# A decode layer on one core: one W_o set loaded as 64 rows, and 48 of 128 score columns by TensorE in the last step

## The chip, the cores and the metric

The kernel runs on one core of one Trainium2 chip. The metric is the device time of one execution in microseconds, as the median of the runs shown. The profile is of one more execution of the same program, read from the first to the last instruction (its span).

## The reference

One token for each of two sequences goes through an attention layer with a key and value cache and then through a gated feed-forward layer, all in bfloat16:

```
q = layernorm(x) @ wq                     # B=2, D=512, 32 heads of 128
scores = q . k_cache / sqrt(128)          # 8192 cached positions per head
p = softmax(scores);  o = p . v_cache
h = x + o @ wo
g = layernorm(h)
out = h + (relu(g @ W_gate) * (g @ W_up)) @ W_down     # F=1376
```

There are 32 key and value heads, one for each query head. The K and V caches are 134 MB each, read once; the weights are some 12 MB. No number of the caches is used twice.

## The kernel before

**Steps.** The work on the caches goes in 32 steps (`steps`), 16 pairs of heads for each of the two sequences. A step takes 4 MB of K and 4 MB of V. Each of the 128 partitions holds 128 consecutive positions (`NT`) of one head: the first 64 partitions have the pair's first head, the other 64 its second. K and V have two buffers each (`kbuf`, `vbuf`), and step i uses buffer i % 2. All loads are issued from SyncE's queue by `load_kv` (line 115): the K of step i+2 after `scores(i)`, the V of step i+1 after the second half of the values of step i-1.

**Scores.** The 128 score columns of a step are shared. The last `NPE` = 32 go through TensorE (`scores_pe`): eight positions' tiles are transposed against an identity (line 268), ScalarE copies the eight from PSUM to SBUF (`kT`, line 269), and eight matmuls with q follow (line 259). There are four such groups, and two copies bring their scores into `scol` (lines 277 and 278). The first `NV` = 96 columns go through VectorE: a product of K with q, which is written over K (`products`, line 286), and in `scores` four halving adds (line 301) and a sum over the last eight elements (line 305). Then come the maximum over the columns (line 310), over the partitions with a matmul (line 312) and a minimum (line 317), and the exponentials on ScalarE (line 320).

**Values.** `values(i, part)` multiplies the probabilities with V in two halves of 16 matmuls (line 336). For the last two steps `values_cols` does it in 128 narrow matmuls (line 359).

**The order.** It is written out by hand (`tc.manual_schedule`): every engine runs its instructions in the order in which the program gives them. In the loop at the end of the kernel's middle part step i gives: `scores_pe(i)`, `products(i)`, `behind(i - 2)`, the first half of the values of step i-1, `scores(i)`, the next K load, the second half of the values, the next V load. In the last step (31) `values_cols(30)` stands between `behind(29)` and `scores(31)`.

**behind.** Some steps close a group of head pairs. For them `sums` adds the exponentials over the partitions with a matmul (line 236, `z_ps`) and takes the reciprocal on VectorE (line 238), and `normalise` scales the group's outputs (line 242). Where the heads of a whole W_o set are then known, `attend_set` multiplies them with W_o.

**W_o.** It lies in `wbig`, where W_q was, in three sets of 16, 8 and 4 heads (`SETS`) and the last four heads by themselves. In a set of n heads each of the 128 partitions holds n consecutive rows of W_o, so that each partition gets one contiguous run of n KB; the loads are at line 196. The heads' outputs must then be brought to the partitions which hold their rows. `attend_set` spreads them with a product (line 373) and a matmul with a pattern of ones (`quot` and `rest`, line 377), copies that to SBUF (line 381), and multiplies with W_o's rows, four matmuls for each row index (line 384). The last four heads are loaded head by head and multiplied by `attend` (line 392).

**The end.** After step 31 there are the last values, the attention's sum with x (line 454), the second layer norm (`ln_cols`), the gate and up products (line 463) and the down product (line 478). W_gate and W_up go into the first K buffer after the last use of that buffer in step 30, and W_down is loaded in four pieces, the last one of 96 rows (64, 24 and 8) in the middle of the run (line 432).

Of the kernel before, what the change touches and what calls it, by code (L numbers as in the profile page):

```python
# [7 lines left out]
ACT = mybir.ActivationFunctionType  # L8
ALU = mybir.AluOpType
# [14 lines left out]
def kernel(  # L24
# [24 lines left out]
    ROW = NT * Dh  # L49
    NG = Hq // 2  # L50
    NPE = NT // 4
    NV = NT - NPE
    TPC = 8
    VG = 4
    EPS = 1e-5
# [5 lines left out]
    FC = 11  # L61


    SETS = [(0, Hq // 2), (Hq // 2, Hq // 4), (3 * Hq // 4, Hq // 8)]
    HM = Hq - Hq // 8

    assert Sq == 1 and Hkv == Hq and Dh == P and D == KC * P and Hq == 32 and NPE % TPC == 0
    assert F == 10 * P + 96

    consts = ctx.enter_context(tc.tile_pool(name="consts", bufs=1))  # L70
# [4 lines left out]

    kbuf = big.tile([P, 2, ROW], bf16)
    vbuf = big.tile([P, 2, ROW], bf16)
    wbig = big.tile([P, KC * Hq * Dh], bf16)
    wd_sb = big.tile([P, FC, D], bf16)
    qrep = consts.tile([P, B, NG, Dh], bf16)  # L80

    wq_sb = wbig.rearrange("p (c n) -> p c n", c=KC)
    wo_sb = wbig.rearrange("p (h n) -> p h n", h=Hq)

    wgu = kbuf[:, 0, 0:2 * KC * F].rearrange("p (k c f) -> p k c f", k=2, c=KC)

# [11 lines left out]
    warm = consts.tile([P, 1], f32)  # L98
    ocol = consts.tile([P, Hq, B], bf16)

    quot = [consts.tile([P, P // n], bf16, name=f"quot{n}") for _, n in SETS]
    rest = [consts.tile([P, n], bf16, name=f"rest{n}") for _, n in SETS]
    orow = [consts.tile([P, n, B], bf16, name=f"orow{n}") for _, n in SETS]
    qT = consts.tile([P, B, Hq], bf16)
    xc = consts.tile([P, B, KC], f32)
    hc = consts.tile([P, B, KC], f32)
# [31 lines left out]
    with tc.manual_schedule():  # L138

        xb = small.tile([P, B, KC], bf16, tag="xb")  # L140
        nc.sync.dma_start(out=xb, in_=_dram(A_x, 0, [[KC, P], [D, B], [1, KC]]))
        nc.sync.dma_start(out=wbig, in_=_dram(A_wq, 0, [[KC * Hq * Dh, P], [1, KC * Hq * Dh]]))
        load_kv(A_k_cache, kbuf, 0, pieces=4)
        load_kv(A_k_cache, kbuf, 1)
        load_kv(A_v_cache, vbuf, 0)
# [46 lines left out]
                nc.scalar.activation(out=qrep[:, b, g0:g0 + 4, :], in_=r_ps, func=ACT.Copy)  # L192


        for h0, n in SETS:
            nc.sync.dma_start(
                out=wbig[:, h0 * D:(h0 + n) * D], in_=_dram(A_wo, h0 * Dh * D, [[n * D, P], [1, n * D]]),
            )
        nc.sync.dma_start(
            out=wo_sb[:, HM:Hq, :], in_=_dram(A_wo, HM * Dh * D, [[D, P], [Dh * D, Hq - HM], [1, D]]),  # L200
        )
        for (h0, n), qu, re in zip(SETS, quot, rest):
            nc.gpsimd.memset(re, 0.0)
            for k in range(P // n):
                nc.gpsimd.affine_select(  # L205
                    out=re, in_=re, compare_op=ALU.not_equal, fill=1.0,
                    base=-k * n, pattern=[[-1, n]], channel_multiplier=1,
                )
            nc.gpsimd.memset(qu, 1.0)
            nc.gpsimd.affine_select(  # L210
                out=qu, in_=qu, compare_op=ALU.is_ge, fill=0.0,
                base=0, pattern=[[-n, P // n]], channel_multiplier=1,
            )
            nc.gpsimd.affine_select(
                out=qu, in_=qu, compare_op=ALU.is_ge, fill=0.0,
                base=n - 1, pattern=[[n, P // n]], channel_multiplier=-1,
            )


# [25 lines left out]

        scols = {}

        def scores_pe(i):
            b, g = steps[i]
            s = i % 2  # L250
            kt = kbuf[:, s, :]

            sc_ps = ps.tile([P, NPE, 2], f32, tag="sc")
            kT = small.tile([P, NPE * P], bf16, tag="kT")

            def times_q(c0):
                for k in range(TPC):
                    t = c0 + k
                    nc.tensor.matmul(  # L259
                        out=sc_ps[:, t, :], lhsT=kT[:, t * P:(t + 1) * P],  # L260
                        rhs=qT[:, b, 2 * g:2 * g + 2], start=True, stop=True,
                    )

            for c0 in range(0, NPE, TPC):
                t_ps = ps2.tile([P, TPC, P], bf16, tag="tp")
                for k in range(TPC):
                    t = NV + c0 + k
                    nc.tensor.transpose(t_ps[:, k, :], kt[:, t * Dh:(t + 1) * Dh], ident)  # L268
                nc.scalar.activation(  # L269
                    out=kT[:, c0 * P:(c0 + TPC) * P], in_=t_ps.rearrange("p t s -> p (t s)"), func=ACT.Copy,  # L270
                )
                if c0:
                    times_q(c0 - TPC)
            times_q(NPE - TPC)
            scol = small.tile([P, NT], f32, tag="scol")
            scols[i] = scol
            nc.scalar.activation(out=scol[0:HALF, NV:NT], in_=sc_ps[0:HALF, :, 0], func=ACT.Copy)  # L277
            nc.scalar.activation(out=scol[HALF:P, NV:NT], in_=sc_ps[HALF:P, :, 1], func=ACT.Copy)

        def products(i):  # L280

            b, g = steps[i]
            kt = kbuf[:, i % 2, :]
            for t0, n in ([(0, 32), (32, 32), (64, 32)] if i == 0 else [(0, NV)]):
                kv = _free(kt, t0 * Dh, [[Dh, n], [1, Dh]])
                nc.vector.tensor_tensor(  # L286
                    out=kv, in0=kv,
                    in1=_free(qrep, (b * NG + g) * Dh, [[0, n], [1, Dh]]), op=ALU.mult,
                )

        def scores(i):

            b, g = steps[i]
            s = i % 2
            kt = kbuf[:, s, :]
            scol = scols[i]
            width = Dh
            while width > 8:
                half = width // 2
                lo = _free(kt, 0, [[Dh, NV], [1, half]])  # L300
                nc.vector.tensor_tensor(  # L301
                    out=lo, in0=lo, in1=_free(kt, half, [[Dh, NV], [1, half]]), op=ALU.add,
                )
                width = half
            nc.vector.tensor_reduce(  # L305
                out=scol[:, 0:NV], in_=_free(kt, 0, [[Dh, NV], [1, 8]]), axis=AXIS.X, op=ALU.add,
            )

            pm = small.tile([P, 1], f32, tag="pm")
            nc.vector.tensor_reduce(out=pm, in_=scol, axis=AXIS.X, op=ALU.max)  # L310
            mx_ps = ps.tile([P, 2, HALF], f32, tag="mx")
            nc.tensor.matmul(  # L312
                out=mx_ps.rearrange("p a b -> p (a b)"), lhsT=_free(pm, 0, [[0, P]]), rhs=nscale,
                start=True, stop=True,
            )
            nm = small.tile([P, 2], f32, tag="nm")
            nc.vector.tensor_reduce(out=nm, in_=mx_ps, axis=AXIS.X, op=ALU.min)  # L317
            for j in range(2):
                r = slice(j * HALF, (j + 1) * HALF)
                nc.scalar.activation(  # L320
                    out=pgz[r, s, :, j, :], in_=scol[r, :].rearrange("p (u t) -> p u t", t=VG), func=ACT.Exp, scale=SCALE,
                    bias=nm[r, j:j + 1], accum_out=zc[r, b, g, j:j + 1],
                )
# [41 lines left out]

        def attend_set(k):

            h0, n = SETS[k]
            or_ps = ps.tile([P, B, n], f32, tag="mx")
            for b in range(B):  # L370
                sp = small.tile([P, P], bf16, tag="spread")
                nq = P // n
                nc.vector.tensor_tensor(
                    out=_free(sp, 0, [[nq, n], [1, nq]]), in0=_free(ocol, h0 * B + b, [[B, n], [0, nq]]),
                    in1=_free(quot[k], 0, [[0, n], [1, nq]]), op=ALU.mult,
                )
                nc.tensor.matmul(
                    out=or_ps[:, b, :], lhsT=sp, rhs=rest[k],
                    start=True, stop=True,
                )  # L380
            nc.scalar.activation(out=orow[k], in_=or_ps.rearrange("p b c -> p c b"), func=ACT.Copy)
            for r in range(n):
                for c in range(KC):
                    nc.tensor.matmul(
                        out=att_ps[:, c, :],
                        lhsT=_free(wo_sb, (h0 + r) * D + c, [[KC, P]]), rhs=orow[k][:, r, :],
                        start=(h0 == 0 and r == 0 and c == 0), stop=False, skip_group_check=True,
                    )

        def attend(h):  # L390
            for c in range(KC):
                nc.tensor.matmul(
                    out=att_ps[:, c, :],
                    lhsT=_free(wo_sb, h * D + c, [[KC, P]]), rhs=ocol[:, h, :],
                    start=False, stop=(h == Hq - 1), skip_group_check=True,
                )

        def behind(i):
# [4 lines left out]
            normalise(i)  # L403
            b, g0, n = groups[i]
            if b == B - 1:
                for k, (h0, m) in enumerate(SETS):
                    if 2 * (g0 + n) == h0 + m:
                        attend_set(k)
                if 2 * g0 >= HM:
                    for h in range(2 * g0, 2 * (g0 + n)):  # L410
                        attend(h)
# [103 lines left out]
```

## Time and profile before

| | |
|---|---|
| Median of 3 runs | 670.48 us (670.46 to 671.56) |
| The profiled execution | 671.36 us |
| Its span | 669.6 us |
| Mean granted TensorE clock | 0.784 of full speed |
| Read from HBM | 281.05 MB, 420 GB/s over the span |
| PE busy | 444.4 us (66%) |
| VectorE (DVE) busy | 478.5 us (71%) |
| ScalarE (ACT) busy | 195.9 us (29%) |
| GpSimd (POOL) busy | 26.2 us (4%) |

The share of busy time is a mean over the span. A line of the timeline or of the chain gives the start in us from the span's start and the length in us; then the engine, the line of the kernel (L286 is line 286), the operation, what it writes and reads with shapes, the count, and in brackets the engine's idle time before it and what ended that. The chain of waits is followed back from the last instruction: at each step to what released it, or to the instruction before it on its engine.

### The profile page before, as it was taken

Reading aid. Unit: us, or ns where it says so; the run is one execution under the profiler, and the core shown is the slowest. Engines: PE = TensorE matmul, PEld = TensorE weight load, DVE = VectorE, ACT = ScalarE, POOL = GpSimd, SP = SyncE. Lnnn points to the kernel's source line nnn. Section 1 sums busy time; section 2 is a strip of 40 time slices with the busy share of each in tenths; the row PEclk is TensorE's granted clock in tenths of the full one; section 3 lists DMA queues with packets and bytes.
Section 4 is the critical chain, followed back from the end, with each engine's and each line's share of the span. In section 5 each row is a group of like instructions: output and inputs, shape, how many; then the busy total and the mean of one; then the engine's idle time right before and its main releaser. Section 6 shows DMA issues by size and latency. Waiting matters only on the chain.

```text
span 669.6 us, 8843 instructions
## 1 busy us (share of the span) xinstructions
PE 444.4 (66%) x3878; PEld 230.3 (34%) x3878; DVE 478.5 (71%) x301; ACT 195.9 (29%) x372; POOL 26.2 (4%) x84
## 2 busy tenths in 40 slices
PE   2563765677666668776656776666776866588655
PEld 2432332333223333332323332333333433343255
DVE  1891788777778767778877776887777788777771
ACT  1531233333212333222233321323331223333130
POOL 7800000000000000000000000000000000000000
PEclk9857678988767788876789877778887767798775
DMA  8999999999999999999999999999999999999994
GB/s 349 433 419 428 437 436 426 431 428 430 437 424 430 415 434 426 439 426 432 428 430 432 431 434 422 435 430 430 430 431 434 428 426 431 438 430 426 427 412 167
DMA packets 12618, 281.62 MB, mean 421 GB/s; under 512 B 1860, under 2 KB 2468, under 8 KB 2980
## 3 DMA queue, kind: packets, MB, share of 16 engines
q1 hardware_dynamic: 12580, 281.06, 98.2%
q8 instruction: 30, 0.49, 0.3%
q14 instruction: 8, 0.07, 0.0%
HBM read 281.05 MB, written 0.00 MB: 420 GB/s over the span
## 4 chain that ended last, share of the span: by engine, by line
DMA 67%; PE 21%; DVE 10%; ACT 1%; issue 0%; SPq 0%; DVEq 0%
DMA vbuf<-in_A_v_cache_dram 53%; PE pv_ps L336 18%; DMA kbuf<-in_A_k_cache_dram 12%; DVE kbuf L301 5%; DVE kbuf L286 4%; DMA wbig<-in_A_wq_dram 2%; PE mx_ps L312 1%; DVE scol L305 1%; ACT kT L269 1%; PE q_ps L176 1%; PE o_ps L359 1%; PE g_ps L463 0%; PE d_ps L478 0%; PE u_ps L463 0%; PE z_ps L236 0%
## 5 line engine op out<-in xcount | busy, mean ns | idle before, releaser
L336 PE MATMUL pv_ps<-vbuf,pgz 128*8 128x512 bf16 x960 | 281.9, 460 | 122.1 <-DMA vbuf<-in_A_v_cache_dram 122.1
L286 DVE TENSOR_TENSOR kbuf<-kbuf,qrep 128x12288 bf16<-128x12288 bf16 (+1 forms) x34 | 210.0, 6181 | 119.7 <-DMA kbuf<-in_A_k_cache_dram 106.7
L301 DVE TENSOR_TENSOR kbuf<-kbuf 128x6144 bf16<-128x6144 bf16 (+3 forms) x128 | 212.1, 1657 | 4.2
L336 PEld LDWEIGHTS <-pgz 128*8 128x8 bf16 x960 | 93.3, 100 | 286.7 <-issue 215.6
L269 ACT ACTIVATE kT<-t_ps 128x1024 bf16<-128x1024 bf16 x128 | 124.2, 1021 | 32.4 <-PE t_ps L268 32.0
L320 ACT ACTIVATE pgz<-scol,nm 64x128 bf16<-64x128 f32 x64 | 25.5, 399 | 327.6 <-DVE nm L317 326.9
L268 PE MATMUL t_ps<-ident,kbuf 128*128 128x128 bf16 x1024 | 77.4, 227 | 16.9 <-DMA kbuf<-in_A_k_cache_dram 16.9
L259 PE MATMUL sc_ps<-qT,kT 128*128 128x2 bf16 x1024 | 45.4, 165 | 48.3 <-ACT kT L269 45.5
L268 PEld LDWEIGHTS <-kbuf 128*128 128x128 bf16 x1024 | 62.4, 102 | 27.4 <-DMA kbuf<-in_A_k_cache_dram 25.6
L259 PEld LDWEIGHTS <-kT 128*128 128x128 bf16 x1024 | 34.7, 97 | 67.5 <-ACT kT L269 67.5
L317 DVE TENSOR_REDUCE nm<-mx_ps 128x2 f32<-128x128 f32 x32 | 9.3, 292 | 39.8 <-PE mx_ps L312 39.8
L343 ACT ACTIVATE pv<-pv_ps 8x512 f32<-8x512 f32 x30 | 17.7, 589 | 64.6 <-PE pv_ps L336 64.6
L305 DVE TENSOR_REDUCE scol<-kbuf 128x96 f32<-128x768 bf16 x32 | 30.5, 953 | 1.1
L312 PE MATMUL mx_ps<-nscale,pm 128*128 128x128 f32 x64 | 16.2, 336 | 7.0 <-DVE pm L310 6.9
L312 PEld LDWEIGHTS mx_ps<-nscale,pm 128*128 128x128 f32 x64 | 9.9, 194 | 20.3 <-issue 11.7
L205 POOL TENSOR_SCALAR_AFFINE_SELECT rest<-rest 128x4 bf16<-128x4 bf16 (+2 forms) x56 | 16.7, 299 | 4.0 <-POOL rest L205 0.2
L348 PE MATMUL o_ps<-pick,pv 128*128 128x8 f32 (+1 forms) x64 | 8.4, 258 | 5.5 <-ACT pv L343 5.5
L320 ACT ACTIVATION_READ_ACCUMULATOR pgz<-scol,nm 64x1 f32 x64 | 11.8, 185 | 0.0
L310 DVE TENSOR_REDUCE pm<-scol 128x1 f32<-128x128 f32 x32 | 9.2, 286 | 3.3
L348 PEld LDWEIGHTS o_ps<-pick,pv 128*128 128x128 f32 x64 | 7.7, 191 | 9.5 <-ACT pv L343 8.3
L277 ACT ACTIVATE scol<-sc_ps 64x32 f32<-64x32 f32 x32 | 6.1, 191 | 14.3 <-PE sc_ps L259 14.3
L176 PE MATMUL q_ps<-xn,wbig 128*128 128x2 bf16 x128 | 3.6, 165 | 8.7 <-DMA wbig<-in_A_wq_dram 8.7
(71 smaller groups left out, 94.5 us busy)
## 6 DMA issues: line engine op xcount, KB each, us to landing
kbuf<-in_A_k_cache_dram SPq DMA_DIRECT2D x31, 4096.0 KB, 24.6
vbuf<-in_A_v_cache_dram SPq DMA_DIRECT2D x31, 4096.0 KB, 29.3
wbig<-in_A_wq_dram SPq DMA_DIRECT2D x1, 4096.0 KB, 12.9
kbuf<-in_A_k_cache_dram SPq DMA_DIRECT2D x4, 1024.0 KB, 18.2
vbuf<-in_A_v_cache_dram SPq DMA_DIRECT2D x4, 1024.0 KB, 18.5
wbig<-in_A_wo_dram SPq DMA_DIRECT2D x1, 2048.0 KB
kbuf<-in_B_W_gate_dram SPq DMA_DIRECT2D x1, 1376.0 KB
kbuf<-in_B_W_up_dram SPq DMA_DIRECT2D x1, 1376.0 KB
```

The costliest lines, as they stand in the source:

```text
L205: nc.gpsimd.affine_select(out=re, in_=re, compare_op=ALU.not_equal, fill=1.0, base=-k * n, pattern=[[-1, n]], channel_multiplier=1,)
L259: nc.tensor.matmul(out=sc_ps[:, t, :], lhsT=kT[:, t * P:(t + 1) * P], rhs=qT[:, b, 2 * g:2 * g + 2], start=True, stop=True,)
L268: nc.tensor.transpose(t_ps[:, k, :], kt[:, t * Dh:(t + 1) * Dh], ident)
L269: nc.scalar.activation(out=kT[:, c0 * P:(c0 + TPC) * P], in_=t_ps.rearrange("p t s -> p (t s)"), func=ACT.Copy,)
L286: nc.vector.tensor_tensor(out=kv, in0=kv, in1=_free(qrep, (b * NG + g) * Dh, [[0, n], [1, Dh]]), op=ALU.mult,)
L301: nc.vector.tensor_tensor(out=lo, in0=lo, in1=_free(kt, half, [[Dh, NV], [1, half]]), op=ALU.add,)
L305: nc.vector.tensor_reduce(out=scol[:, 0:NV], in_=_free(kt, 0, [[Dh, NV], [1, 8]]), axis=AXIS.X, op=ALU.add,)
L312: nc.tensor.matmul(out=mx_ps.rearrange("p a b -> p (a b)"), lhsT=_free(pm, 0, [[0, P]]), rhs=nscale, start=True, stop=True,)
L320: nc.scalar.activation(out=pgz[r, s, :, j, :], in_=scol[r, :].rearrange("p (u t) -> p u t", t=VG), func=ACT.Exp, scale=SCALE, bias=nm[r, j ...
L336: nc.tensor.matmul(out=pv_ps[i][r, :], lhsT=pgz[:, s, u].rearrange("p j t -> p (j t)"), rhs=vbuf[:, s, u * VG * Dh:(u + 1) * VG * Dh], sta ...
L343: nc.scalar.activation(out=pv[r, w], in_=pv_ps[i][r, :], func=ACT.Copy)
L348: nc.tensor.matmul(out=o_ps[i][:, 0:2 * n], lhsT=pv[:, w, t * Dh:(t + 1) * Dh], rhs=pick[:, t, first % 4:first % 4 + n].rearrange("p k j - ...
```

## The change

Two things are changed, with what they need.

The set of 8 heads is laid on 64 partitions: each holds 16 rows of W_o instead of 8. A set is now described by its first head, its number of heads, the partitions it lies on and its first column in `wbig`, and `SROWS` gives the rows in a partition (16, 16 and 4). In the load of the 64-partition set, DRAM rows are taken in the order of an outer dimension of eight and an inner one of eight, so that the transfer's source has eight as its slowest dimension. The spread's pattern and the matmuls of `attend_set` follow: the sums are over 64 partitions, and there are 16 row indices instead of 8. `wbig` becomes 40 x 512 columns wide instead of 32 x 512, and the last four heads lie from column 36 x 512 on.

In the last step 48 columns of scores go through TensorE and 80 through VectorE (`NPE_LAST`, `share`); in the others it remains 32 and 96. The tile `kT` of a whole step becomes one tile for each group of eight, of which there are four buffers.

```diff
-    NV = NT - NPE
+    NPE_LAST = 3 * NT // 8
...
-    SETS = [(0, Hq // 2), (Hq // 2, Hq // 4), (3 * Hq // 4, Hq // 8)]
+    SETS = [(0, 16, P, 0), (16, 8, HALF, 20), (24, 4, P, 16)]
+    WO_T = 36
...
-    wbig = big.tile([P, KC * Hq * Dh], bf16)
+    wbig = big.tile([P, 40 * D], bf16)
...
+    SROWS = [n * Dh // w for _, n, w, _ in SETS]
+    quot = [consts.tile([P, Dh // r], bf16, name=f"quot{k}") for k, r in enumerate(SROWS)]
+    rest = [consts.tile([P, r], bf16, name=f"rest{k}") for k, r in enumerate(SROWS)]
+    orow = [consts.tile([P, r, B], bf16, name=f"orow{k}") for k, r in enumerate(SROWS)]
...
-        for h0, n in SETS:
+        for (h0, n, w, at), r in zip(SETS, SROWS):
+            rows = [[r * D, w]] if w == P else [[r * D, 8], [8 * r * D, w // 8]]
             nc.sync.dma_start(
-                out=wbig[:, h0 * D:(h0 + n) * D], in_=_dram(A_wo, h0 * Dh * D, [[n * D, P], [1, n * D]]),
+                out=wbig[0:w, at * D:(at + r) * D], in_=_dram(A_wo, h0 * Dh * D, rows + [[1, r * D]]),
             )
...
-        for (h0, n), qu, re in zip(SETS, quot, rest):
+        for r, qu, re in zip(SROWS, quot, rest):
             nc.gpsimd.memset(re, 0.0)
-            for k in range(P // n):
+            for k in range(P // r):
...
+        def share(i):
+
+            npe = NPE_LAST if i == N - 1 else NPE
+            return NT - npe, npe
+
         def scores_pe(i):
...
-            kT = small.tile([P, NPE * P], bf16, tag="kT")
+            kTs = {}
...
-            for c0 in range(0, NPE, TPC):
+            for c0 in range(0, npe, TPC):
                 t_ps = ps2.tile([P, TPC, P], bf16, tag="tp")
                 for k in range(TPC):
-                    t = NV + c0 + k
+                    t = nv + c0 + k
                     nc.tensor.transpose(t_ps[:, k, :], kt[:, t * Dh:(t + 1) * Dh], ident)
-                nc.scalar.activation(
-                    out=kT[:, c0 * P:(c0 + TPC) * P], in_=t_ps.rearrange("p t s -> p (t s)"), func=ACT.Copy,
-                )
+                kTs[c0] = small.tile([P, TPC * P], bf16, tag="kT", name="kT", bufs=4)
+                nc.scalar.activation(out=kTs[c0], in_=t_ps.rearrange("p t s -> p (t s)"), func=ACT.Copy)
...
-                lo = _free(kt, 0, [[Dh, NV], [1, half]])
+                lo = _free(kt, 0, [[Dh, nv], [1, half]])
...
         def attend_set(k):
 
-            h0, n = SETS[k]
-            or_ps = ps.tile([P, B, n], f32, tag="mx")
+            h0, n, w, at = SETS[k]
+            r = SROWS[k]
+            nq = Dh // r
+            or_ps = ps.tile([P, B, r], f32, tag="mx")
             for b in range(B):
                 sp = small.tile([P, P], bf16, tag="spread")
-                nq = P // n
                 nc.vector.tensor_tensor(
-                    out=_free(sp, 0, [[nq, n], [1, nq]]), in0=_free(ocol, h0 * B + b, [[B, n], [0, nq]]),
+                    out=_free(sp, 0, [[nq, n], [1, nq]] if w == P else [[1, n], [8, nq]]),
+                    in0=_free(ocol, h0 * B + b, [[B, n], [0, nq]]),
                     in1=_free(quot[k], 0, [[0, n], [1, nq]]), op=ALU.mult,
                 )
...
-            for r in range(n):
+            for c0 in range(r):
                 for c in range(KC):
                     nc.tensor.matmul(
                         out=att_ps[:, c, :],
-                        lhsT=_free(wo_sb, (h0 + r) * D + c, [[KC, P]]), rhs=orow[k][:, r, :],
-                        start=(h0 == 0 and r == 0 and c == 0), stop=False, skip_group_check=True,
+                        lhsT=_free(wbig[0:w], (at + c0) * D + c, [[KC, P]]), rhs=orow[k][0:w, c0, :],
+                        start=(k == 0 and c0 == 0 and c == 0), stop=False, skip_group_check=True,
                     )
```

More of the change, by code (lines that the diff above doesn't have):

```diff
@@ L61 @@
     FC = 11
-    SETS = [(0, Hq // 2), (Hq // 2, Hq // 4), (3 * Hq // 4, Hq // 8)]
+    SETS = [(0, 16, P, 0), (16, 8, HALF, 20), (24, 4, P, 16)]
+    WO_T = 36
     HM = Hq - Hq // 8
-    assert Sq == 1 and Hkv == Hq and Dh == P and D == KC * P and Hq == 32 and NPE % TPC == 0
+    assert Sq == 1 and Hkv == Hq and Dh == P and D == KC * P and Hq == 32 and NPE % TPC == NPE_LAST % TPC == 0
     assert F == 10 * P + 96
@@ L77 @@
     vbuf = big.tile([P, 2, ROW], bf16)
-    wbig = big.tile([P, KC * Hq * Dh], bf16)
+    wbig = big.tile([P, 40 * D], bf16)
     wd_sb = big.tile([P, FC, D], bf16)
     qrep = consts.tile([P, B, NG, Dh], bf16)
-    wq_sb = wbig.rearrange("p (c n) -> p c n", c=KC)
-    wo_sb = wbig.rearrange("p (h n) -> p h n", h=Hq)
+    wq_sb = wbig[:, 0:KC * Hq * Dh].rearrange("p (c n) -> p c n", c=KC)
     wgu = kbuf[:, 0, 0:2 * KC * F].rearrange("p (k c f) -> p k c f", k=2, c=KC)
@@ L99 @@
     ocol = consts.tile([P, Hq, B], bf16)
-    quot = [consts.tile([P, P // n], bf16, name=f"quot{n}") for _, n in SETS]
-    rest = [consts.tile([P, n], bf16, name=f"rest{n}") for _, n in SETS]
-    orow = [consts.tile([P, n, B], bf16, name=f"orow{n}") for _, n in SETS]
+    SROWS = [n * Dh // w for _, n, w, _ in SETS]
+    quot = [consts.tile([P, Dh // r], bf16, name=f"quot{k}") for k, r in enumerate(SROWS)]
+    rest = [consts.tile([P, r], bf16, name=f"rest{k}") for k, r in enumerate(SROWS)]
+    orow = [consts.tile([P, r, B], bf16, name=f"orow{k}") for k, r in enumerate(SROWS)]
     qT = consts.tile([P, B, Hq], bf16)
@@ L141 @@
         nc.sync.dma_start(out=xb, in_=_dram(A_x, 0, [[KC, P], [D, B], [1, KC]]))
-        nc.sync.dma_start(out=wbig, in_=_dram(A_wq, 0, [[KC * Hq * Dh, P], [1, KC * Hq * Dh]]))
+        nc.sync.dma_start(out=wbig[:, 0:KC * Hq * Dh], in_=_dram(A_wq, 0, [[KC * Hq * Dh, P], [1, KC * Hq * Dh]]))
         load_kv(A_k_cache, kbuf, 0, pieces=4)
@@ L192 @@
                 nc.scalar.activation(out=qrep[:, b, g0:g0 + 4, :], in_=r_ps, func=ACT.Copy)
-        for h0, n in SETS:
+        for (h0, n, w, at), r in zip(SETS, SROWS):
+            rows = [[r * D, w]] if w == P else [[r * D, 8], [8 * r * D, w // 8]]
             nc.sync.dma_start(
-                out=wbig[:, h0 * D:(h0 + n) * D], in_=_dram(A_wo, h0 * Dh * D, [[n * D, P], [1, n * D]]),
+                out=wbig[0:w, at * D:(at + r) * D], in_=_dram(A_wo, h0 * Dh * D, rows + [[1, r * D]]),
             )
         nc.sync.dma_start(
-            out=wo_sb[:, HM:Hq, :], in_=_dram(A_wo, HM * Dh * D, [[D, P], [Dh * D, Hq - HM], [1, D]]),
+            out=wbig[:, WO_T * D:(WO_T + Hq - HM) * D].rearrange("p (h n) -> p h n", n=D),
+            in_=_dram(A_wo, HM * Dh * D, [[D, P], [Dh * D, Hq - HM], [1, D]]),
         )
-        for (h0, n), qu, re in zip(SETS, quot, rest):
+        for r, qu, re in zip(SROWS, quot, rest):
             nc.gpsimd.memset(re, 0.0)
-            for k in range(P // n):
+            for k in range(P // r):
                 nc.gpsimd.affine_select(
                     out=re, in_=re, compare_op=ALU.not_equal, fill=1.0,
-                    base=-k * n, pattern=[[-1, n]], channel_multiplier=1,
+                    base=-k * r, pattern=[[-1, r]], channel_multiplier=1,
                 )
@@ L211 @@
                 out=qu, in_=qu, compare_op=ALU.is_ge, fill=0.0,
-                base=0, pattern=[[-n, P // n]], channel_multiplier=1,
+                base=0, pattern=[[-r, P // r]], channel_multiplier=1,
             )
@@ L215 @@
                 out=qu, in_=qu, compare_op=ALU.is_ge, fill=0.0,
-                base=n - 1, pattern=[[n, P // n]], channel_multiplier=-1,
+                base=r - 1, pattern=[[r, P // r]], channel_multiplier=-1,
             )
@@ L251, in scores_pe @@
             kt = kbuf[:, s, :]
-            sc_ps = ps.tile([P, NPE, 2], f32, tag="sc")
-            kT = small.tile([P, NPE * P], bf16, tag="kT")
+            nv, npe = share(i)
+            sc_ps = ps.tile([P, npe, 2], f32, tag="sc")
+            kTs = {}
             def times_q(c0):
                 for k in range(TPC):
-                    t = c0 + k
                     nc.tensor.matmul(
-                        out=sc_ps[:, t, :], lhsT=kT[:, t * P:(t + 1) * P],
+                        out=sc_ps[:, c0 + k, :], lhsT=kTs[c0][:, k * P:(k + 1) * P],
                         rhs=qT[:, b, 2 * g:2 * g + 2], start=True, stop=True,
                     )
-            for c0 in range(0, NPE, TPC):
+            for c0 in range(0, npe, TPC):
                 t_ps = ps2.tile([P, TPC, P], bf16, tag="tp")
                 for k in range(TPC):
-                    t = NV + c0 + k
+                    t = nv + c0 + k
                     nc.tensor.transpose(t_ps[:, k, :], kt[:, t * Dh:(t + 1) * Dh], ident)
-                nc.scalar.activation(
-                    out=kT[:, c0 * P:(c0 + TPC) * P], in_=t_ps.rearrange("p t s -> p (t s)"), func=ACT.Copy,
-                )
+                kTs[c0] = small.tile([P, TPC * P], bf16, tag="kT", name="kT", bufs=4)
+                nc.scalar.activation(out=kTs[c0], in_=t_ps.rearrange("p t s -> p (t s)"), func=ACT.Copy)
                 if c0:
                     times_q(c0 - TPC)
-            times_q(NPE - TPC)
+            times_q(npe - TPC)
             scol = small.tile([P, NT], f32, tag="scol")
             scols[i] = scol
-            nc.scalar.activation(out=scol[0:HALF, NV:NT], in_=sc_ps[0:HALF, :, 0], func=ACT.Copy)
-            nc.scalar.activation(out=scol[HALF:P, NV:NT], in_=sc_ps[HALF:P, :, 1], func=ACT.Copy)
+            nc.scalar.activation(out=scol[0:HALF, nv:NT], in_=sc_ps[0:HALF, :, 0], func=ACT.Copy)
+            nc.scalar.activation(out=scol[HALF:P, nv:NT], in_=sc_ps[HALF:P, :, 1], func=ACT.Copy)
         def products(i):
@@ L283, in products @@
             kt = kbuf[:, i % 2, :]
-            for t0, n in ([(0, 32), (32, 32), (64, 32)] if i == 0 else [(0, NV)]):
+            nv, _ = share(i)
+            for t0, n in ([(0, 32), (32, 32), (64, 32)] if i == 0 else [(0, nv)]):
                 kv = _free(kt, t0 * Dh, [[Dh, n], [1, Dh]])
@@ L296, in scores @@
             scol = scols[i]
+            nv, _ = share(i)
             width = Dh
@@ L299, in scores @@
                 half = width // 2
-                lo = _free(kt, 0, [[Dh, NV], [1, half]])
+                lo = _free(kt, 0, [[Dh, nv], [1, half]])
                 nc.vector.tensor_tensor(
-                    out=lo, in0=lo, in1=_free(kt, half, [[Dh, NV], [1, half]]), op=ALU.add,
+                    out=lo, in0=lo, in1=_free(kt, half, [[Dh, nv], [1, half]]), op=ALU.add,
                 )
@@ L305, in scores @@
             nc.vector.tensor_reduce(
-                out=scol[:, 0:NV], in_=_free(kt, 0, [[Dh, NV], [1, 8]]), axis=AXIS.X, op=ALU.add,
+                out=scol[:, 0:nv], in_=_free(kt, 0, [[Dh, nv], [1, 8]]), axis=AXIS.X, op=ALU.add,
             )
@@ L366, in attend_set @@
         def attend_set(k):
-            h0, n = SETS[k]
-            or_ps = ps.tile([P, B, n], f32, tag="mx")
+            h0, n, w, at = SETS[k]
+            r = SROWS[k]
+            nq = Dh // r
+            or_ps = ps.tile([P, B, r], f32, tag="mx")
             for b in range(B):
                 sp = small.tile([P, P], bf16, tag="spread")
-                nq = P // n
                 nc.vector.tensor_tensor(
-                    out=_free(sp, 0, [[nq, n], [1, nq]]), in0=_free(ocol, h0 * B + b, [[B, n], [0, nq]]),
+                    out=_free(sp, 0, [[nq, n], [1, nq]] if w == P else [[1, n], [8, nq]]),
+                    in0=_free(ocol, h0 * B + b, [[B, n], [0, nq]]),
                     in1=_free(quot[k], 0, [[0, n], [1, nq]]), op=ALU.mult,
                 )
[L377 to L381, printed above, removed]
-            for r in range(n):
+                nc.tensor.matmul(out=or_ps[0:w, b, :], lhsT=sp[:, 0:w], rhs=rest[k], start=True, stop=True)
+            nc.scalar.activation(
+                out=orow[k][0:w], in_=or_ps[0:w].rearrange("p b c -> p c b"), func=ACT.Copy,
+            )
+            for c0 in range(r):
                 for c in range(KC):
@@ L393, in attend @@
                     out=att_ps[:, c, :],
-                    lhsT=_free(wo_sb, h * D + c, [[KC, P]]), rhs=ocol[:, h, :],
+                    lhsT=_free(wbig, (WO_T + h - HM) * D + c, [[KC, P]]), rhs=ocol[:, h, :],
                     start=False, stop=(h == Hq - 1), skip_group_check=True,
@@ L405, in behind @@
             if b == B - 1:
-                for k, (h0, m) in enumerate(SETS):
+                for k, (h0, m, _, _) in enumerate(SETS):
                     if 2 * (g0 + n) == h0 + m:
```

## The prediction

> **What bounds the kernel now.** First the page: the span, the slices, the queues and the chain that ended last.
>
> ```profile
> span 669.6 us, 8843 instructions
> ...
> DMA  8999999999999999999999999999999999999994
> ...
> q1 hardware_dynamic: 12580, 281.06, 98.2%
> q8 instruction: 30, 0.49, 0.3%
> ...
> DMA 67%; PE 21%; DVE 10%; ACT 1%; issue 0%; SPq 0%; DVEq 0%
> ```
>
> The sixteen transfer engines are full in every slice but the first and last, so bytes set the time up to the last K and V. Two questions remain: when does the slowest engine finish the last loads, and how long is the work behind them? For the second I read the chain of waits in order of time near the end.
>
> ```profile
> 593.62 30.27 DMA vbuf<-in_A_v_cache_dram
> 623.89 0.04 issue
> 623.93 6.25 PE pv_ps L336 x16
> ...
> 635.88 0.48 PE t_ps L268 x8
> 636.36 0.02 issue
> 636.38 3.88 ACT kT L269 x4
> 640.27 0.04 issue
> 640.31 0.35 PE sc_ps L259 x8
> 640.67 0.24 PE z_ps L236 x2
> ...
> 641.71 3.28 DVE kbuf L301
> ```
>
> From the landing of V of step 29 (at 623.89) on, nothing is slack: pv_ps, the last step's transposes, four kT copies back to back on ACT, then z_ps, and DVE's adds of the last step after it. Last the timeline of DVE, to see what it waits for there.
>
> ```profile
> 633.64 6.56 DVE L286 TENSOR_TENSOR kbuf<-kbuf,qrep 128x12288 bf16<-128x12288 bf16 x1 [2.71 <-DMA kbuf<-in_A_k_cache_dram]
> ...
> 640.93 0.18 DVE L238 RECIPROCAL rz<-z_ps 128x4 f32<-128x4 f32 x1 [0.74 <-PE z_ps L236]
> ...
> 663.72 1.60 PE L478 MATMUL d_ps<-hm,wd_sb 96*128 96x2 bf16 x44 [0.40 <-DVE hm L473]
> ```
>
> DVE's products end at 640.20; DVE then sits idle 0.74 us for z_ps, which stands on PE behind the transposes and their products. In the last step TensorE's branch, not DVE's, is already the longer.
>
> The first question needs the trace's own records. Each transfer leaves a landing mark for each engine that carries a share; sorted, they tell how far the engines stand apart. The last K load (issued at 608.9) has marks at 627.32 plus 0, 0.15, 0.16, 0.21, 0.79, 0.84, 2.00, 2.25, 4.57, 4.62, 4.65, 4.69, 4.86, 5.02, 6.21 and 6.29. So there are eight early and eight late engines, and the core waits for the last. The late ones are late because of the 30 instruction fetches (q8): after each, one mark moves by about 1.55 (at 265.3 from 1.77 to 3.33), and they go in turn over the same eight engines.
>
> **Part one: the W_o set of 8 heads.** Before, 128 rows of 8 KB over sixteen engines: 8 packets each, 0.313 us a packet, 2.50 us. After, 64 rows of 16 KB; the source's outer dimension is 8. The only transfer of eight rows before is W_down's last piece: it has 8 marks and one more at its issue, so it used eight engines. I take the same eight, with 8 packets of 16 KB each at 0.614 (rows of the 16-head set): 4.91 us. These eight become 2.41 us later, the other eight 2.50 earlier, for the rest of the run.
>
> Which are they? The eight-row piece landed at 228.71, 228.72, 228.80, 229.43, 229.59, 229.77, 230.41 and 230.47. Following each engine's packets (the next starts 3 to 4 ns before the last one ends), six belong to the early half and two, ninth and tenth of the sixteen in the V load before it (1.53 and 1.62 behind the first), to the late half. Late engines at 1.5 to 1.6 that get two more fetches of 1.55 stand at 4.6 to 4.7 by the last K: the marks 4.57 to 4.69. So the new last mark is 4.69 + 2.41 = 7.10, against 6.29 for K and 6.28 for V of step 29. **The last landing becomes 0.82 us later**; the relieved late engines fall to 3.8 and the early ones rise to 2.25 + 2.41 = 4.7. Bounds: if the late two were not among the eight, 2.98 + 2.41 (an early engine after its fetch at 632.5) is the most, 0.9 us earlier; if the very last engine were one, 2.41 us later. I take 0.82, as the two are placed by their packets.
>
> Do early engines run dry? The last K was issued at 608.9 and the first engine began it at 617.6: 8.7 us in hand, less 2.5 and 0.8. No.
>
> [...]
>
> **Part two: reading that set.** attend_set(1), in step 29, has 64 matmuls instead of 32 on 64 rows. The 32 before took 1.20 us at 601.70; 1.2 more end at 604.1, and the next pv_ps began at 604.40, held by V. Hidden, with the later V too; 1.2 if that cover went. The spread has a strided write: 0.283 us each before, in the worst case twice that; DVE waits 1.42 us for mx_ps later in that step, which hides it.
>
> **Part three: the last step.** PE gets 16 transposes and 16 products more and ACT two copies; the four copies took 3.88 us without a gap, so two more take 1.94, and z_ps comes 1.94 later (bounds 1.94 and 2.05, at the page's 1021 ns each). DVE's products shrink by 2048 of 12288 elements, about 1.07 us, but that only lengthens DVE's wait for z_ps from 0.74 to some 3.8 us: no gain. Behind z_ps DVE's adds shrink. Rows by shape: 3072 elements 1.757, 1536 elements 0.957, so 0.52 ns an element; 1024 + 512 + 256 + 128 fewer make 1.00 us, and the reduce (953 ns for 768, 128 fewer at 1.04 ns) 0.13. **Net 1.94 - 1.13 = 0.81 us later.** Queued behind the longer PE stretch are or_ps, attend_set(2) and values_cols(30), which ended at 646.96; mx_ps needed PE at 649.88, so it has 2.9 us for 1.94.
>
> **Free edits.** The two scol copies take 48 columns instead of 32 (0.19 us, DVE's adds run beside them). The split kT tiles: a copy reuses the tile of four copies earlier, whose products ended two copies before, so no wait. GpSimd has 8 selects fewer (0.19 each) in the first 25 us, and nobody reads them before 522. W_o remains four issues. PE gets 64 instructions more in step 29 and 64 in the last, half a fetch; the fetches after 601 come earlier, in the same turn, and next in turn are six other engines before the two in question. What comes behind shifts as a whole: W_down's last mark was 663.43 with d_ps at 663.72; now 656.88 + 4.68 + 2.41 = 663.97 against 665.3. Hidden.
>
> **Sum.** 0.82 + 0.81 = 1.63 us. The profiled execution took 671.36 us (span 669.6 and 1.76 around it), so 672.99; it stands 0.88 above the median of 670.48, so the median becomes 672.1.
>
> **Rivals.**
> - The transfer relieves the late engines (not slower). If fewer than the two late engines I name carry it, the last landing is 0.9 us earlier, part three's 0.81 remains: -0.1, 670.4. It decides from where the loaded engines' old lag at the last K is below 6.29 - 2.41 - 0.81 = 3.07. For it: six of eight are early. Against: the two marks at 230.41 and 230.47.
> - The set is spread over all sixteen, or the landing is covered: part three alone, 671.3. Against it: the chain hangs on V's landing at 623.89.
> - PE's clock. It is granted at full rate from 629.3 to 643.0 and at half after that. If the heavier step loses it earlier, transposes slow down: mx_ps took 0.49 at full and 0.78 at half, a factor 1.6; 0.61 us for 8 transposes becomes 0.97, with 0.4 for products that is 1.37 against ACT's 0.97, 0.4 more for each of six groups: 2.4 more, 674.5.
> - DVE's shorter step counts in full: it needs z_ps before the products end, 3.8 us earlier than I have it; then 1.07 + 0.74 + 1.13 = 2.9 less, with the landing 0.82 later: 668.4. Only a change of PE's order would do that, and there is none.
>
> **How the numbers follow.** About 0.2% (1.3 us) is what a measurement can tell from no change. Forecast 0.52, its own range 671.4 (both engines at the mark 4.57, so 0.69 for the landing, and half of the 1.1 us over which the three runs spread) to 673.1 (an 8 KB instruction fetch on one of the two engines: that at 632.5 moved a mark from 2.00 to 2.98); a quarter of it lies within 0.2%. First rival 0.15 (a third of that faster), second 0.15, clock 0.10, DVE 0.08. Faster 0.08 + 0.05 = 0.13; slower 0.39 + 0.10 + 0.02 = 0.51; the rest, 0.36, same. The range from 669.5 to 673.6 leaves out DVE's case and the clock's.
>
> **What would show it.** The last K's products start near 634.5 instead of 633.64. Six kT copies take 5.8 us, and DVE waits 3 to 4 us for z_ps. Adds and reduce take about 5.7 us. The last marks of K and V stand 7.1 behind the first, the late six under 4.2. I am wrong if the marks close up (the first rival), or if the loaded set's 16 KB packets are on all engines.

## The result and the profile after

The changed kernel takes 676.5 us (median of 6 runs, 674.92 to 681.58), the kernel before 670.58 (6 runs, 670.46 to 671.56) on the same chip: a ratio of 1.0091, 95% interval 1.007 to 1.0112. It is 5.9 us slower where 1.6 were forecast (672.1), outside the range given (669.5 to 673.6). The profiled execution took 676.74 us, with a span of 674.9. A few executions here ran 5 to 10 us longer than the others of their kernel; in the two of them that were profiled (of the kernel with two transfers below, and of the changed kernel on the second chip) every transfer took 12% longer for some 80 us, so medians are compared.

First the page of the changed kernel: the span, the slices of the transfer engines, the queues, and the chain that ended last by engine.

```profile
span 674.9 us, 8958 instructions
...
DMA  8999999999999999999999999999999999999992
GB/s 348 439 384 347 433 434 435 433 434 432 431 434 430 419 433 435 434 432 432 432 430 432 431 431 434 431 430 432 433 434 435 432 432 433 430 432 424 429 414 79
...
q1 hardware_dynamic: 12508, 281.06, 97.7%
q8 instruction: 31, 0.51, 0.3%
...
DMA 66%; PE 18%; DVE 14%; ACT 1%; issue 0%; SPq 0%; DVEq 0%; ACTq 0%
```

The engines are as busy as before, but in the third and fourth slice, from 34 to 67 us, they move 384 and 347 GB/s. The W_o loads lie there. From the fifth slice to the last but one the rate is 414 to 435, as it was before, so what was lost is not made up: the engines had no slack for it.

Then the chain of waits near the end (start, length, engine, what).

```profile
599.34 29.88 DMA vbuf<-in_A_v_cache_dram
629.27 5.00 PE pv_ps L346 x16
...
638.91 1.06 PE o_ps L358 x8
639.97 0.48 PE t_ps L277 x8
640.47 3.88 ACT kT L279 x4
...
644.41 0.87 ACT kT L279
...
645.33 1.03 ACT kT L279
...
646.40 0.35 PE sc_ps L268 x8
646.75 0.24 PE z_ps L240 x2
...
647.79 2.75 DVE kbuf L311
650.57 1.50 DVE kbuf L311
652.09 0.84 DVE kbuf L311
652.95 0.50 DVE kbuf L311
```

V of step 29 lands at 629.22, 5.33 us later than before (623.89). That alone is the slowdown; the rest is nearly a draw. The first half of pv_ps takes 5.00 instead of 6.25, as TensorE's full clock is granted 2.8 us behind its start and not 5.4 (o_ps is 4.08 later). The copies take 5.87 from first to last instead of 3.88, so z_ps is 6.1 later. The four adds take 5.59 instead of 6.59 and the reduce 0.83 instead of 0.96. The last instruction starts at 670.46 instead of 665.35, 5.11 later.

The timeline shows what VectorE waits for in the last step, and the down product.

```profile
638.90 5.49 DVE L295 TENSOR_TENSOR kbuf<-kbuf,qrep 128x10240 bf16<-128x10240 bf16 x1 [3.88 <-DMA kbuf<-in_A_k_cache_dram]
647.02 0.18 DVE L242 RECIPROCAL rz<-z_ps 128x4 f32<-128x4 f32 x1 [2.62 <-PE z_ps L240]
...
668.82 1.60 PE L489 MATMUL d_ps<-hm,wd_sb 96*128 96x2 bf16 x44 [0.40 <-DVE hm L484]
```

The products are 1.07 us shorter and buy only a longer wait, 2.62 instead of 0.74. d_ps waits for VectorE alone: W_down's last mark was at 667.96.

**Where the time went.** The windows of the two kernels over the W_o loads (the stretch and its length, busy time of PE, PEld, DVE, ACT and POOL, granted clock, share of the transfer engines, GB/s). Before:

```profile
48.00:52.00 4.00, 4.00 (x17) 1.49 (x16) 2.24 (x5) 0.84 (x4) 0.00 (x0) 0.87 1.00 394
52.00:56.00 4.00, 2.26 (x11) 0.72 (x9) 0.00 (x0) 0.73 (x3) 0.00 (x0) 1.00 1.10 441
56.00:60.00 4.00, 0.00 (x0) 0.00 (x0) 0.00 (x0) 0.00 (x0) 0.00 (x0) 0.91 1.10 475
```

After:

```profile
48.00:52.00 4.00, 4.00 (x18) 1.56 (x17) 1.73 (x4) 0.98 (x4) 0.00 (x0) 0.95 1.16 252
52.00:56.00 4.00, 1.91 (x9) 0.61 (x7) 0.00 (x0) 0.59 (x1) 0.00 (x0) 1.00 0.93 200
56.00:60.00 4.00, 0.00 (x0) 0.00 (x0) 0.00 (x0) 0.00 (x0) 0.00 (x0) 0.83 1.00 338
```

Busy engines, half the rate. The 64-row set leaves eight landing marks, from 56.79 to 60.35, where before the set of 8 heads left sixteen, from 50.04 to 51.78. The trace's records of single packets say how the rate fell. Between 48 and 58 us a 16 KB packet of the 64-row set takes 1.26 us (median of 53), where those of the 16-head set took 0.611 just before. The other transfers under way, which lie on 128 partitions, are slowed as well: 4 KB packets 0.30 instead of 0.16, 1 KB 0.085 instead of 0.047, and the 32 KB packets of the next K 2.01 instead of 1.22. From 60 us on they are as before (0.046, 0.159 and 1.213 up to 64 us).

### The profile page after: what moved, and what is told of

It reads as the page before. It is cut to its first block, busy times and chain, and to the rows that moved or that the text cites. A ratio compares the mean times of both kernels' runs of the same rounds, so it can differ in the third digit from the quotient of the medians.

```text
span 674.9 us, 8958 instructions
## 1 busy us (share of the span) xinstructions
PE 445.4 (66%) x3942; PEld 233.1 (35%) x3942; DVE 476.6 (71%) x301; ACT 197.9 (29%) x374; POOL 14.1 (2%) x76
## 4 chain that ended last, share of the span: by engine, by line
DMA 66%; PE 18%; DVE 14%; ACT 1%; issue 0%; SPq 0%; DVEq 0%; ACTq 0%
DMA vbuf<-in_A_v_cache_dram 44%; DMA kbuf<-in_A_k_cache_dram 20%; PE pv_ps L346 14%; DVE kbuf L311 7%; DVE kbuf L295 6%; DMA wbig<-in_A_wq_dram 2%; DVE scol L315 1%; ACT kT L279 1%; PE mx_ps L322 1%; PE q_ps L178 1%; PE o_ps L369 1%; PE g_ps L474 0%; PE d_ps L489 0%; PE u_ps L474 0%; PE z_ps L240 0%
## 5 line engine op out<-in xcount | busy, mean ns | idle before, releaser
L346 PE MATMUL pv_ps<-vbuf,pgz 128*8 128x512 bf16 x960 | 278.6, 456 | 118.9 <-DMA vbuf<-in_A_v_cache_dram 118.9
L295 DVE TENSOR_TENSOR kbuf<-kbuf,qrep 128x12288 bf16<-128x12288 bf16 (+2 forms) x34 | 208.9, 6150 | 126.2 <-DMA kbuf<-in_A_k_cache_dram 113.8
L311 DVE TENSOR_TENSOR kbuf<-kbuf 128x6144 bf16<-128x6144 bf16 (+4 forms) x128 | 211.3, 1651 | 4.2
L279 ACT ACTIVATE kT<-t_ps 128x1024 bf16<-128x1024 bf16 x130 | 126.4, 1021 | 41.4 <-PE t_ps L277 40.8
L277 PE MATMUL t_ps<-ident,kbuf 128*128 128x128 bf16 x1040 | 79.6, 228 | 25.0 <-DMA kbuf<-in_A_k_cache_dram 24.9
L277 PEld LDWEIGHTS <-kbuf 128*128 128x128 bf16 x1040 | 63.9, 102 | 35.6 <-DMA kbuf<-in_A_k_cache_dram 34.3
L315 DVE TENSOR_REDUCE scol<-kbuf 128x96 f32<-128x768 bf16 (+1 forms) x32 | 30.4, 949 | 1.1
L285 ACT ACTIVATE scol<-sc_ps 64x32 f32<-64x32 f32 (+1 forms) x32 | 6.1, 191 | 14.4 <-PE sc_ps L268 14.4
L209 POOL TENSOR_SCALAR_AFFINE_SELECT rest<-rest 128x4 bf16<-128x4 bf16 (+1 forms) x48 | 9.2, 193 | 3.4 <-POOL rest L207 0.2
```

The source lines that it names most:

```text
L279: nc.scalar.activation(out=kTs[c0], in_=t_ps.rearrange("p t s -> p (t s)"), func=ACT.Copy)
L295: nc.vector.tensor_tensor(out=kv, in0=kv, in1=_free(qrep, (b * NG + g) * Dh, [[0, n], [1, Dh]]), op=ALU.mult,)
L311: nc.vector.tensor_tensor(out=lo, in0=lo, in1=_free(kt, half, [[Dh, nv], [1, half]]), op=ALU.add,)
L315: nc.vector.tensor_reduce(out=scol[:, 0:nv], in_=_free(kt, 0, [[Dh, nv], [1, 8]]), axis=AXIS.X, op=ALU.add,)
L346: nc.tensor.matmul(out=pv_ps[i][r, :], lhsT=pgz[:, s, u].rearrange("p j t -> p (j t)"), rhs=vbuf[:, s, u * VG * Dh:(u + 1) * VG * Dh], sta ...
```

## The experiments

Each runs beside the kernel before on the same chip, and its ratio is to that; the loads and the last step are changed, never what is computed. The first theory was that eight engines are too few for the set, or that they read DRAM badly; its rival that the engines meet where they write.

**The W_o layout alone, and the last step alone.** The first is the changed kernel with

```diff
-    NPE_LAST = 3 * NT // 8
+    NPE_LAST = NT // 4
```

and the second the changed kernel with the old sets:

```diff
-    SETS = [(0, 16, P, 0), (16, 8, HALF, 20), (24, 4, P, 16)]
-    WO_T = 36
+    SETS = [(0, 16, P, 0), (16, 8, P, 16), (24, 4, P, 24)]
+    WO_T = 28
```

> Only the W_o set on 64 rows by eight engines; the last step keeps 32 and 96 columns. If the set's load is what costs (its 16 KB packets took 1.25 us instead of 0.61 between 48 and 58 us, and the others' packets took twice their time too), this alone is 5.0 us slower than before, 675.6, and V of step 29 lands near 629. If the two edits only cost together, it is within 1 us of before.

> Only the last step's 48 columns by TensorE (and the split kT tiles); the W_o set of 8 heads stays on 128 rows and sixteen engines. By my step for it: two more copies 1.94 us, adds and sum 1.13 less, so 0.81 us slower, 671.4; DVE waits about 3.3 us for z_ps after its products. If the last step's share is a rival cause of the loss, 2 us or more slower.

Measured: the layout alone 674.25 against 671.35, ratio 1.0038 (1.0024 to 1.0052), 2.9 us where 5.0 were expected; its 16 KB packets take 1.25 too, and V of step 29 lands at 626.94. The last step alone 672.22, ratio 1.0011 (1.0003 to 1.002), 0.87 us where 0.81 was forecast. VectorE's line of the latter:

```profile
633.85 5.49 DVE L295 TENSOR_TENSOR kbuf<-kbuf,qrep 128x10240 bf16<-128x10240 bf16 x1 [2.65 <-DMA kbuf<-in_A_k_cache_dram]
643.19 0.18 DVE L242 RECIPROCAL rz<-z_ps 128x4 f32<-128x4 f32 x1 [3.85 <-PE z_ps L240]
```

3.85 us for z_ps, as the prediction had it ("some 3.8"). So the last step went as reckoned, and the miss lies in the load. But the two add up to 3.8, not to 5.4 or 5.9; that comes back below.

**The same 64 rows by sixteen engines, and by two transfers of 32 rows.** The first gives the source sixteen as its outer dimension, with four neighbouring partitions to each of the sixteen. The second keeps eight, and the order in which DRAM is read, but loads rows 0 to 31 and then 32 to 63, so that in either transfer there are four neighbouring partitions to each of the eight. The pattern of the spread follows in both; the last step is the old one.

```diff
-            rows = [[r * D, w]] if w == P else [[r * D, 8], [8 * r * D, w // 8]]
+            rows = [[r * D, w]] if w == P else [[r * D, 16], [16 * r * D, w // 16]]
```

```diff
+            for p0, p1 in [(0, w)] if w == P else [(0, 32), (32, 64)]:
+                rows = [[r * D, w]] if w == P else [[r * D, 8], [8 * r * D, 4]]
...
+                    out=wbig[p0:p1, at * D:(at + r) * D],
+                    in_=_dram(A_wo, h0 * Dh * D + p0 * r * D, rows + [[1, r * D]]),
```

> The set on the same 64 rows, but with an outer dimension of 16, so that sixteen engines carry 4 packets of 16 KB each; the last step as before. [...] Theory eight (it is the use of eight engines): packets 0.61 us, time as before, 670.6. Theory source order (engines read 16 KB pieces that lie side by side in DRAM): packets slow, 673 or more.

> The set on the same 64 rows by eight engines, in the same DRAM order, but as two transfers of 32 rows, in each of which an engine has 4 neighbouring rows instead of 8. [...] Theories eight and source order: packets 1.25 us as in the changed kernel, 5 us slower, 675.6.

Measured: with sixteen engines 16 KB packets still take 1.25. The ten runs lie between 670.45 and 678.51 (median 672.17, ratio 1.0046, 1.0018 to 1.0074), too far apart for the time to price the load. The profiled execution, the fastest, does: its last mark of V of step 29 is at 623.93, and at 620.52 in the kernel before with K and V at the same address (below), 3.4 us earlier, where four packets alone would make 2.6. With two transfers of 32 rows the packets take 0.611, all of them, and the time is 669.14 (ratio 0.9959, 0.9943 to 0.9974): 5.1 us less than the layout in one transfer. Its windows:

```profile
48.00:52.00 4.00, 4.00 (x17) 1.52 (x16) 1.69 (x4) 0.93 (x4) 0.00 (x0) 0.89 1.04 429
52.00:56.00 4.00, 2.17 (x11) 0.70 (x8) 0.00 (x0) 0.64 (x2) 0.00 (x0) 1.00 1.15 472
56.00:60.00 4.00, 0.00 (x0) 0.00 (x0) 0.00 (x0) 0.00 (x0) 0.00 (x0) 0.89 1.01 434
```

So neither the eight engines nor the order in DRAM slows the packets: this kernel has both. What the two slow kernels share, and this one lacks, is a single transfer to all 64 rows. That two engines at a time then meet where they write is the author's reading; the packets' records do not name rows, and no run shows which rows would meet. The packet times fit it: two packets of 16 KB in 1.25 us are 26.2 GB/s, one in 0.611 is 26.8. The 5.1 us agree with the eight packets of a loaded engine, 8 x (1.25 - 0.614) = 5.1, and with the profiles: the first K load behind the W_o loads has its last mark at 71.22 with one transfer and at 65.92 with two.

**The set on 128 rows, by eight engines.** The old layout of the set, 8 KB a partition, but eight as the outer dimension, with sixteen neighbouring partitions to each of the eight; the last step is the old one.

```diff
-    SETS = [(0, 16, P, 0), (16, 8, HALF, 20), (24, 4, P, 16)]
+    SETS = [(0, 16, P, 0), (16, 8, P, 20), (24, 4, P, 16)]
...
-            rows = [[r * D, w]] if w == P else [[r * D, 8], [8 * r * D, w // 8]]
+            rows = [[r * D, w]] if h0 != 16 else [[r * D, 8], [8 * r * D, w // 8]]
```

> The set of 8 heads on all 128 rows, but by eight engines, 16 neighbouring rows of 8 KB for each; last step and start address as before. [...]

Measured: 680.38 against 671.25, ratio 1.0135 (1.0118 to 1.0152), 9.1 us. 8 KB packets take 0.90 instead of 0.313, 4 KB packets 0.49, 32 KB packets 3.29.

```profile
48.00:52.00 4.00, 4.00 (x14) 1.39 (x13) 2.15 (x5) 0.33 (x2) 0.00 (x0) 0.72 0.99 144
52.00:56.00 4.00, 2.80 (x13) 0.96 (x11) 0.00 (x0) 1.24 (x5) 0.00 (x0) 1.00 1.24 176
56.00:60.00 4.00, 0.00 (x0) 0.00 (x0) 0.00 (x0) 0.00 (x0) 0.00 (x0) 0.63 0.97 149
```

So it is not the number of rows either: all 128 are used, and it is worse. A packet takes not twice as long, as the 16 KB ones did (1.25 for 0.611), but almost three times. For a loaded engine that makes 16 x (0.90 - 0.313) = 9.4; measured are 9.1, of which some 1.1 belong to the shift between the engines (next section). Why it is three times here, and why in the changed kernel the engines that do not carry the set are slowed as well, none of these runs shows.

**An unused tile of 32 bytes.** The kernel with two transfers is 2.2 us faster than the kernel before, which nothing in it explains, and by its records the 32 KB packets of K and V take 1213 ns where before they took 1216 or 1224. `quot`, `rest` and `orow` of the changed sets take 32 bytes of a partition more than the old ones, and everything that is placed behind them, K and V among it, moves by 32: from 32736 to 32768. So one line goes into the kernel before, and into the kernel with two transfers, which it puts 32 off again.

```diff
     qT = consts.tile([P, B, Hq], bf16)
+    pad = consts.tile([P, 16], bf16, name="pad")
```

> The kernel before with one unused tile of 32 bytes a partition ahead of the big buffers, so that they start at byte 32768 of a partition instead of 32736. In the changed kernel the smaller tables of the W_o sets moved them in just this way, and its 32 KB packets take 1213 ns instead of 1216, 9.67 us a transfer instead of 9.72. Theory start address: this alone makes the last landing some 3.1 us earlier, 668.2 against 671.3. Theory that the 1213 has another cause (the chip, the profile): time as before, 671.3.

> The two transfers of 32 rows once more, with the 32 bytes added, so that the big buffers start 32 bytes past a multiple of 64, as in the kernel before. Theory start address: it loses the 3.1 us that the version without the tile had, and only the shift of 2.4 us between the engines is left: 0.8 us slower than before, 672.1, by my step for the landing. Rival: the two transfers are faster by themselves, 669.1 again.

Measured: the kernel before with the tile 667.64 against 671.34, ratio 0.9948 (0.9936 to 0.9961), 3.7 us faster. From 100 to 200 us, 32 KB packets take 1215.1 ns on average instead of 1220.2, a load of 4 MB 9.67 us instead of 9.72, and some 66 such loads make the 3.4 by which the last K comes earlier. Its chain of waits no longer hangs on V of step 29:

```profile
606.20 23.98 DMA kbuf<-in_A_k_cache_dram
630.20 6.56 DVE kbuf L287
636.76 0.10 DVE rz L239
```

The other way round, two transfers with K and V 32 off take 672.47, ratio 1.0018 (1.001 to 1.0027): 1.1 us slower than before. (Its K and V start at 32800; no other offset was tried.) This is the shift between engines with K and V off by 32 as before and with normal packets, for which 0.82 was forecast. Its last mark of V of step 29 is at 625.06 against 623.89, and the last two of the sixteen marks stand 9.78 and 9.81 behind the first, the next at 7.03: two late engines in the loaded eight, as forecast.

**The changed kernel again, on another chip.**

> The changed kernel beside the kernel before on the chip that ran the experiments. If the four parts add up (the set's slow load, 674.25 - 669.14 = 5.1; the shift between the engines, 1.2; the last step, 0.9; the start address, -3.7), it is 3.5 us slower than before, 674.9. If it is 5.9 slower, as on the first chip, the two edits cost some 2.4 us more together than one by one.

Measured: 676.61 against 671.25, ratio 1.0106 (1.0054 to 1.0158), 5.4 us. The terms so far are -3.7 for the address, +1.1 for the shift, +5.1 for the slow load and +0.9 for the last step, together 3.4. About 2 us are left. The traces show them in the landing of V of step 29. The layout alone:

```profile
598.50 28.44 DMA vbuf<-in_A_v_cache_dram
626.94 0.04 issue
```

It lands at 626.94 there and at 629.22 in the changed kernel. The first engine is even 0.75 earlier in the latter (616.90 against 617.65), but the last stands 12.32 behind it instead of 9.29. Half of that gap, 1.55 us, is an instruction fetch: in both kernels a last mark jumps by 1.55 more than a load takes (11.2 instead of 9.67) each time the latest engine has fetched. In the changed kernel it happens with the V loads issued at 422.8 and 599.3 (and at 428.6 and 605.2 on the second chip), in the layout alone at 246.9, 441.9 and 619.1, the last of them one V load too late to count. The fetches' own durations, which repeat every eight, say the same: from the seventeenth on they are 958, 879, 881, 934 ns in the changed kernel, 947, 879, 886, 934 in its run on the second chip, and 960, 951, 879, 879, 938 in the layout alone, one place later. So the turn in which engines fetch was the same in both runs of one program and another in the other program, and in the changed kernel the latest engine's turn falls on the load that counts. Why the turn differs was not found. The rest of the 2.28 us between the two landings, 0.7, is older: the last mark of the first K load behind the W_o loads stands at 72.25 in the changed kernel and at 71.22 in the layout alone, with the same W_o loads in both. Its cause is open.

**z_ps ahead of the last step's transposes.** The forecast let VectorE's shorter step count "only by a change of PE's order". This is that change, on the kernel with the last step alone; then the same with the 32-byte tile. `sums_pe` issues the z_ps matmul of step 29, which `sums` issued before.

```diff
         for i in range(N):
+            if i == N - 1:
+                sums_pe(i - 2)
             scores_pe(i)
```

> The last step's 48 columns by TensorE, W_o as before, and one thing moved: the matmul of the sums of step 29 (z_ps) stands on PE ahead of the last step's transposes instead of behind them. If the wait for z_ps is what eats DVE's shorter step, DVE now runs its adds right after its products, some 3.3 us earlier than in the version with 48 columns alone, and the time is bounded next by values_cols(30), which PE runs until 647.5: 2.4 us faster than before, 669.0. If DVE waits for something else, 672.2 as with 48 columns alone.

> The same with the 32 bytes ahead of the big buffers. If start address and order add up: 3.1 and 2.4 us, 665.9. If the earlier landings only let DVE wait for V of step 30, no more than one of the two.

Measured: 670.1 against 671.34, ratio 0.9983 (0.9974 to 0.9993), 1.2 us faster than before and 2.1 faster than without the move (672.22); with the tile 666.09, ratio 0.9925 (0.9912 to 0.9939), 5.2 us faster than before and the fastest of all kernels here. The forecast for the first was 1.1 us too low, and its timeline says why:

```profile
633.53 5.49 DVE L302 TENSOR_TENSOR kbuf<-kbuf,qrep 128x10240 bf16<-128x10240 bf16 x1 [3.19 <-DMA kbuf<-in_A_k_cache_dram]
638.94 0.18 DVE L249 RECIPROCAL rz<-z_ps 128x4 f32<-128x4 f32 x1
...
653.26 1.01 PE L376 MATMUL o_ps<-pgz,vbuf 128*128 128x2 bf16 x32 [0.68 <-DMA vbuf<-in_A_v_cache_dram]
...
659.97 1.71 PE L483 MATMUL u_ps<-hn,kbuf 128*128 128x2 bf16 x44 [0.26 <-DMA kbuf<-in_B_W_up_dram]
```

VectorE waits for z_ps no more, and its adds start 4.2 us earlier. But now the last values wait 0.68 for the last quarter of V, and the up product 0.26 for W_up: 0.94 given back to transfers that were hidden before. With the tile the chain of waits ends on W_up:

```profile
631.10 25.33 DMA kbuf<-in_B_W_up_dram
656.43 0.05 issue
656.48 1.73 PE u_ps L484 x44
```

By this chain, a faster last step would have little left to gain.

## Why the prediction was wrong

The sum by its own terms:

| Term | Forecast | Measured | By |
|---|---|---|---|
| The load itself, packets of the set | 0 | +5.1 | one transfer against two |
| Shift between engines | +0.82 | +1.1 | two transfers, old address |
| The last step | +0.81 | +0.9 | the last step alone |
| Start address of K and V | 0 | -3.7 | the tile of 32 bytes |
| Last engine, changed kernel against the layout alone | 0 | about +2.3 (1.55 a fetch, 0.7 open) | marks of V of step 29 |
| Sum | +1.63 | +5.7 | 5.9 and 5.4 on two chips |

- **Part one, the W_o set of 8 heads: the step that failed.** "8 packets of 16 KB each at 0.614" took the price from a transfer of another shape. It was 1.25, and other transfers were slowed with it (32 KB packets 2.01 instead of 1.22). The part had bounds for which engines carry the set, and none for what a packet costs. Sixteen as the outer dimension would not have helped: the kernel with it has the same slow packets (1.25), the one with eight in two transfers has not (0.611).
- **Part one, the shift.** Right in kind: eight engines, two late ones among them, no engine ran dry, and 1.1 for 0.82. The sign it named, a last mark "7.1 behind the first", was wrong, since relieved early engines become the new first: with two transfers and the old offset the last mark of V of step 29 is 9.81 behind the new first, and 7.45 behind where the first stood before.
- **Free edits: failed twice.** They were judged by instructions alone, and the sizes of the tables are not among them. The tables moved K and V by 32 bytes, worth -3.7, more than either term of the sum. And "the fetches after 601 come earlier, in the same turn" looked at the last fetches alone, while the turn differed over the whole run; the forecast's own range allowed for a smaller fetch, of 0.98, and the one that counted cost 1.55.
- **Part two: held in the time, not in its reason.** The 64 matmuls take 2.26 us instead of 1.20, but they start later, at 607.67, and the next pv_ps begins right behind them at 609.86 though its V landed at 608.32: the cover went. It costs nothing because the pv_ps after that waits for V of step 29 until 629.22 in any case.
- **Part three: held.** +1.99 for the copies (1.94), -1.00 and -0.13 for adds and reduce (the same), the wait for z_ps 3.85 in the kernel with this part alone (3.8). In the changed kernel the clock added a part that was not in the sum: -1.25 in pv_ps, where a later V meets an earlier full clock.
- **The rivals.** Relief and a spread set did not occur. PE's clock went the other way: it stayed at full rate through all six groups (granted from 632.1 to 649.2). That VectorE's step counts only if PE's order changes was right, and the kernel with that order shows it; the full gain would have needed earlier weights as well.

The chance of slower, 0.51, was the largest, but for 1.6 us and not for 5.9. The range failed because three terms that were put at zero (the packets, the address and the fetch) are each larger than either that was reckoned. The miss was kept down by luck: without the -3.7 of the address, the terms add up to 9.4.

## What to carry to other kernels

Here the duration of a packet did not hold for another shape of transfer (16 KB in 0.611 and in 1.25 us): when a load is laid on fewer partitions, look at the durations of its packets, and if they are longer than those of other transfers, try it cut into transfers of 32 rows (0.611 again here). In a kernel that is bound by transfers, an edit that changes the size of any tile can move all buffers behind it: compare start addresses, and try a 32-byte pad (3.7 us of 671 here) before reading anything into half a per cent. And when the work behind the last load gets shorter, look up first when the next transfers land.

## What was not expected of the hardware

- In one transfer to 64 partitions, by eight engines or by sixteen, 16 KB packets take 1.25 us each instead of 0.611; in two transfers of 32 partitions they take 0.611. No run here shows why. With eight engines on 128 rows 8 KB take 0.90 instead of 0.313.
- Such a load slows the transfers beside it too: 32 KB packets 2.01 us instead of 1.22 beside the 64-row set, 3.29 beside the 128-row one.
- 32 bytes in the start address of the K and V buffers (32736 or 32768) change the rate of their loads by 0.4% (1220.2 against 1215.1 ns for 32 KB), 3.7 us of 671.
- After an instruction fetch its engine's landing mark is 1.55 us later (11.2 us behind the last one instead of 9.67) and stays so in the loads that follow, and which engine's turn it is differs between programs that differ only in the last step: 1.55 us here.
